# One recorded order for all engines up to the sixth MoE position

## The chip, the core and the metric

The kernel runs on one NeuronCore of a Trainium2 chip. The core has five engines that work side by side, each through its own list of instructions in order: TensorE (PE, matrix products and transposes; its weight loads are shown apart as PEld), VectorE (DVE), ScalarE (ACT), GpSimd (POOL) and SyncE (SP), which here issues all DMA transfers. The engines wait for each other through semaphores. The metric is the time of one execution on the device in microseconds; lower is better.

## What is computed

Banded attention over 2 batches, 8 heads, 768 positions of 64, and then two feed-forward layers over 1536 tokens. All of it is float32.

```python
k_sum = k.reshape(B, H, nb, 32, D).max(axis=3)     # 24 block maxima of K
v_sum = v.reshape(B, H, nb, 32, D).mean(axis=3)    # 24 block means of V
scores_l = scale * q @ k.T, kept where |i - j| < 16
scores_s = scale * q @ k_sum.T + log(32)
a = softmax(concat(scores_l, scores_s)) ; attn = a @ concat(v, v_sum)
x = attn as [1536, 512]
x = ((x @ w_a) * (x @ w_b)) @ w_out                # d_ff 1536, "moe"
h = x @ w_in ; out = (h - tanh(h)) @ w_out2        # d_ff 2048, "moe2"
```

The two weight sets arrive as 8-byte words per element (512 KB for a unit of 128 x 512 weights) and are turned into float32 on the chip.

## The kernel before

**Attention units.** The attention is cut into 24 units of 64 positions (all heads), 12 per batch. A unit's steps are T1 (transpose q, one T1 for two units), W (copy the band of 96 keys and the 24 block maxima into one tile), T2 (scores on TensorE, minimum and mask on VectorE, exponentials on ScalarE), T2b (divide by the sum), T3 (transpose the weights) and T4 (outputs on TensorE; ScalarE writes the high half into the x tile, VectorE subtracts for the low half). Eight units fill the x tile of one token block of 512.

**MoE positions.** The first feed-forward layer runs as a list of positions, `pos`, for three token blocks: for each of 12 groups f of 128 columns there is a product a (`pos_a`, 12 matmuls), a product b (`pos_b`, 12 matmuls, then VectorE multiplies a by b) and, one group later, an output product o (`pos_o`, 12 matmuls into four accumulators). The list begins a0 b0 a1 b1 o0 a2 b2 o1 a3. Each float32 operand is split in a high and a low half, and a product is made of three matmuls: gh and gl are the halves of a times b, and `wsp` holds those of a weight. Twelve matmuls of 128 x 512 belong to a position.

**Weights.** A position needs one weight unit. A unit is loaded into a buffer (three `stage` buffers, and x21a and x21b), decoded and split. The decode is two operations on ScalarE (`dec_a`: da and db), a clamp on GpSimd (dc), and a shift-and-mask (dd), a merge (de) and an add (df) on VectorE; the split is a copy on ScalarE (sh) and a subtraction (sl). When the add is done the buffer is free, and the next unit's load is issued on the SP queue.

**What sets the order.** The start is a recorded order: the string `SEQ` lists the steps of units 0 to 7 of the attention and the decodes and splits of the first three weights, and `op()` writes each step's instructions; `tc.manual_schedule` keeps them as they stand on each engine. A second recorded part follows for all engines but TensorE (loads for units 8 to 10 and `W(8)` to `W(11)`, two early key chunk loads). From position 0 on, `run_plan(j)` adds the planned steps of position j (decodes, attention of later units, key chunks of the second batch, V chunks), weights are split three positions ahead, and a scheduler orders the instructions of all engines but SP, whose order is kept as written up to position 72.

Names in the rows: XA and XB are the x tiles, kt the transposed keys, `w` and `vw` are pools of small tiles, ps, pt, pa, pb and acc are banks of the matmul memory. Lines of the page are those of the kernel before: L370 is in `proj` (products a and b), L398 in `pos_o`, L184 and L185 the split, L161, L164 and L165 dd, de and df, and L755, L757 and L759 the same steps in the recorded part; L601 is a copy on VectorE in the recorded part, L672 its masked minimum, L685 and L686 the sums, L720 and L722 the output halves; L386 multiplies a by b, L363 and L364 write gh and gl; L223, L269, L327 and L340 are the transposes of key chunks, T1, T3 and the outputs T4 of units from 8 on; L141 and L143 load weights, L258 loads V for a unit.

## Time and profile before

| what | before |
|---|---|
| median of three runs | 659.42 us (659.05 to 659.43) |
| the profiled execution | 659.97 us, span 658.2 us |
| TensorE busy | 637.4 us, 97% of the span |
| VectorE busy | 501.9 us, 76% |
| ScalarE busy | 475.1 us, 72% |
| GpSimd busy | 209.1 us, 32% |
| DMA traffic | 62.11 MB, 94 GB/s on average |

The profile is of one execution, by the hardware profiler, so it stands beside the median of the runs and not for it. Busy is the time that an engine's instructions took; matmuls overlap and their ends are modelled. A wait is put down to the engine whose result came last. The clock column of a stretch is the TensorE clock that was granted, as a share of full speed.

### The profile page before, as it was taken

How to read it: one execution, taken by the hardware profiler on the slowest of the kernel's cores; microseconds unless marked ns; L12 is line 12 of the kernel's file. 1: busy time of each engine (PE TensorE's matmuls, PEld its weight loads, DVE VectorE, ACT ScalarE, POOL GpSimd, SP SyncE). 2: the span in 40 equal slices, each digit the busy share in tenths (PEclk: the TensorE clock that was granted, in tenths of full speed). 3: DMA queues.
4: the chain of work that ended last, by engine and by line, in shares of the span. 5: the costliest groups of instructions: out<-in, count | busy, mean ns of one | idle time of the engine just before them, and what ended most of it. 6: DMA issues, size and time to landing. Idle time of an engine off the chain costs nothing.

```text
span 658.2 us, 9626 instructions
## 1 busy us (share of the span) xinstructions
PE 637.4 (97%) x3240; PEld 518.2 (79%) x3240; DVE 501.9 (76%) x999; ACT 475.1 (72%) x1000; POOL 209.1 (32%) x221
## 2 busy tenths in 40 slices
PE   7779999999799999999999999999999999999997
PEld 5567876888588888888888888888888888888885
DVE  5889999898675777747877749777777877777775
ACT  4899886897686787645655548777777777777774
POOL 6752231222000011100111134554444554444441
PEclk9979999999999999999999999999999999999999
DMA  9996984563324554513444200000010000010001
GB/s 203 242 240 185 249 224 127 176 214 116 81 89 124 164 161 141 154 54 113 143 145 145 80 1 0 1 0 1 1 64 1 0 1 0 26 40 1 1 0 64
DMA packets 84781, 62.11 MB, mean 94 GB/s; under 512 B 51892, under 2 KB 75444, under 8 KB 84732
## 3 DMA queue, kind: packets, MB, share of 16 engines
q1 hardware_dynamic: 84732, 61.50, 33.3%
q8 instruction: 25, 0.41, 0.3%
q14 instruction: 24, 0.20, 0.1%
HBM read 54.00 MB, written 7.34 MB: 93 GB/s over the span
## 4 chain that ended last, share of the span: by engine, by line
PE 83%; DVE 8%; ACT 4%; DMA 2%; issue 2%; SPq 1%; POOL 0%; DVEq 0%; ACTq 0%
PE acc L459 20%; PE pb L370 18%; PE pa L370 17%; PE acc L398 12%; PE pt L370 5%; PE ps L370 5%; PE ps L288 1%; DVE w L164 1%; PE ps L340 1%; DVE wsp L185 1%; DMA stage<-in_moe_w_in_dram 1%; DVE w L165 1%; PE pt L240 1%; PE pt L327 1%; SPq L610 1%
## 5 line engine op out<-in xcount | busy, mean ns | idle before, releaser
L185 POOL TENSOR_TENSOR wsp<-w,wsp 128x512 fp32r<-128x512 f32 x97 | 127.4, 1330 | 140.0 <-ACT wsp L184 140.0
L184 ACT ACTIVATE wsp<-w 128x512 fp32r<-128x512 f32 x201 | 121.3, 622 | 17.8 <-PE acc L398 8.0
L185 DVE TENSOR_TENSOR wsp<-w,wsp 128x512 fp32r<-128x512 f32 x104 | 73.9, 712 | 41.0 <-ACT wsp L184 40.8
L179 POOL TENSOR_SCALAR w<-w 128x512 f32<-128x512 f32 x52 | 41.8, 809 | 181.7 <-ACT w L154 168.9
L398 PE MATMUL acc<-gh,wsp 128*128 128x512 f32 x288 | 96.5, 394 | 1.2 <-ACT gh L363 1.2
L370 PE MATMUL pa<-XA,wsp 128*128 128x512 f32 x336 | 85.2, 402 | 2.1 <-ACT XA L720 2.1
L370 PE MATMUL pb<-XA,wsp 128*128 128x512 f32 x336 | 83.9, 393 | 1.4 <-DVE tg L386 1.4
L459 PE MATMUL acc<-wsp,gh 128*128 128x512 f32 x256 | 78.8, 389 | 0.0
L370 PEld LDWEIGHTS pa<-XA,wsp 128*128 128x128 f32 x336 | 64.1, 193 | 16.6 <-ACT XA L720 2.4
L370 PEld LDWEIGHTS pb<-XA,wsp 128*128 128x128 f32 x336 | 62.1, 188 | 14.9 <-ACT x21a L155 1.7
L363 ACT ACTIVATE gh<-tg 128x512 fp32r<-128x512 f32 x68 | 42.4, 624 | 33.9 <-DVE tg L386 33.6
L398 PEld LDWEIGHTS acc<-gh,wsp 128*128 128x128 f32 x288 | 53.7, 188 | 11.9 <-ACT gh L363 1.3
L370 PE MATMUL pb<-XB,wsp 128*128 128x512 f32 x240 | 60.8, 396 | 0.0
L370 PE MATMUL pa<-XB,wsp 128*128 128x512 f32 x240 | 60.0, 394 | 0.0
L398 PE MATMUL acc<-gl,wsp 128*128 128x512 f32 x144 | 56.8, 396 | 1.1 <-DVE gl L364 1.1
L459 PEld LDWEIGHTS acc<-wsp,gh 128*128 128x128 f32 x256 | 48.1, 188 | 9.9
L364 DVE TENSOR_TENSOR gl<-tg,gh 128x512 fp32r<-128x512 f32 x68 | 46.8, 688 | 9.1 <-ACT gh L363 8.9
L370 PEld LDWEIGHTS pa<-XB,wsp 128*128 128x128 f32 x240 | 44.5, 188 | 9.4 <-DVE XB L348 0.2
L370 PEld LDWEIGHTS pb<-XB,wsp 128*128 128x128 f32 x240 | 44.4, 188 | 9.2
L459 PE MATMUL acc<-wsp,gl 128*128 128x512 f32 x128 | 49.8, 389 | 0.0
L459 PE MATMUL acc<-wsp,vw 128*128 128x512 f32 x192 | 46.5, 391 | 0.0
L459 PEld LDWEIGHTS acc<-wsp,vw 128*128 128x128 f32 x192 | 35.9, 188 | 8.2 <-ACT vw L363 0.4
(304 smaller groups left out, 1175.5 us busy)
## 6 DMA issues: line engine op xcount, KB each, us to landing
stage<-in_moe_w_out_dram SPq DMA_DIRECT2D x19, 512.0 KB, 3.5
stage<-in_moe_w_in_dram SPq DMA_DIRECT2D x16, 512.0 KB, 5.6
stage<-in_moe_w_a_dram SPq DMA_DIRECT2D x8, 512.0 KB, 5.0
w<-wsc SPq DMA_DIRECT2D x16, 256.0 KB, 3.4
vw<-in_v_dram SPq DMA_DIRECT2D x19, 192.0 KB, 3.0
stage<-in_moe_w_b_dram SPq DMA_DIRECT2D x7, 512.0 KB, 5.6
wsc<-x21a SPq DMA_DIRECT2D x8, 256.0 KB, 5.1
wsc<-x21b SPq DMA_DIRECT2D x8, 256.0 KB, 4.9
```

The lines of the kernel that those rows point to most:

```text
L164: nc.vector.scalar_tensor_tensor(r, t[:, :, 1], -0x40000000, r, op0=ALU.bitwise_and, op1=ALU.bitwise_or)
L165: nc.vector.tensor_tensor(r, r, t[:, :, 0], op=ALU.add)
L179: nc.gpsimd.tensor_scalar(rf, rf, HI_HI, HI_LO, op0=ALU.min, op1=ALU.max)
L184: nc.scalar.activation(s[:, 0, :], r, AF.Copy)
L185: eng.tensor_tensor(s[:, 1, :], r, s[:, 0, :].bitcast(F32), op=ALU.subtract)
L240: mm(pp, mavg[:, NB - 4 - 4 * c : 2 * NB - 4 - 4 * c], vch.pop(c).rearrange("p h d -> p (h d)"), start=(c == 0), stop=(c == NC - 1),)
L288: mm(pp[:, p, 0:NK], qt[:, p, :], kw[:, p, :], start=True, stop=True)
L363: nc.scalar.activation(dst[0], src, AF.Copy)
L364: eng.tensor_tensor(dst[1], src, dst[0].bitcast(F32), op=ALU.subtract)
L370: mm(dst, w, xx, start=(kk == 0 and n == 0), stop=(kk == KC - 1 and n == 2))
L398: mm(acc[blk][d][:, c0:c1], w, t, start=(f == 0 and c0 == 0 and n == 0), stop=(f == F1 - 1 and n == 2))
L459: mm(a[c], g[:, cs], s[:, i, :], start=(f == 0 and n == 0), stop=(f == F2 - 1 and n == 2))
```

## The change

The recorded part becomes longer and holds all engines, TensorE too. `HEAD_P = 6` positions (a0 b0 a1 b1 o0 a2) are written out as steps M0 to M5 with their evictions (Ma copies a product a, Mt multiplies a by b, Mh and Ml write gh and gl). `HEAD_W = 10` weights are decoded there instead of three, and splits are recorded for the first nine instead of three. Units 8 and 9 of the attention are in the recorded order (unit 9 up to its division), and so are the first three key chunks of the second batch (KP transposes, KE copies, KR takes maxima) and the loads Lk, Lc (V chunks) and LV8 to LV11. The scheduler takes over at position 6.

Besides the order, some steps go to another engine. The copies of the block means of V for units 0 to 7 (`VCE`) were two on ScalarE, two on VectorE and four on GpSimd, and are five on VectorE and three on GpSimd. The add of the decode (`ADD`) was on GpSimd for the first weight, and now is for the second and third; the split's subtraction (`SPL`) was on GpSimd for two weights, and now is for three. W(8) to W(11) stood together on ScalarE ahead of the first product; W(8) and W(9) now stand near the start and W(10) and W(11) among the products.

On the SP queue the first q tile is issued ahead of the last K tile, the first weight (Lw0) right behind the second q tile, and the second weight behind the three V tiles. A buffer that a decode frees is no longer reloaded at once: its name goes into `freed`, and the step Lw with the next number issues the load where it stands in the order.

```diff
     HALF, WARM, VM, PK, KS = 0, 3, 3, -3, 2
+    HEAD_W, HEAD_P = 10, 6
...
-    REG = {0:{ET.SP},72:None}
+    REG = {6:{ET.SP},72:None}
...
     for i, u in enumerate(dseq):
-        if i < LOOK:
+        if i < HEAD_W:
             continue
...
-        plan(ja, dec_a, u)
-        plan(ja + 1, dec_b_next, i)
+        plan(max(ja, HEAD_P), dec_a, u)
+        plan(max(ja + 1, HEAD_P), dec_b_next, i)
...
     for c in range(NC):
-        plan(PK + KS * c, lambda c=c: load_k(1, c, st([128, H, D], "w", 3 * F1)))
-        plan(PK + KS * c + 4, prep_k, 1, c, "ps" if c % 2 else "pt")
+        if c == 5:
+            plan(PK + KS * c, lambda c=c: load_k(1, c, st([128, H, D], "w", 3 * F1)))
+        if c >= 3:
+            plan(PK + KS * c + 4, prep_k, 1, c, "ps" if c % 2 else "pt")
...
-    T3E, WE, ADD, SPL, VCE = 'DDDDADDD', 'PPDPPDPP', 'PDD', 'PPD', 'APPPAPDD'
+    T3E, WE, ADD, SPL, VCE = 'DDDDDDAD', 'DPDPPPPP', 'DPPDDDDDDD', 'PPPDDDDDD', 'DDDDDPPP'
...
+        elif k == "M":
+            fn, g, u = pos[i]
+            x, sp = X[0], wsp.pop(u)
+            if fn is pos_o:
+                fn(g, sp)
+            else:
+                P_["M", i] = pt("pa" if fn is pos_a else "pb")
+                proj(P_["M", i], sp, x)
+        elif k == "Ma":
+            j = (0, 2, 5)[i]
+            ab[pos[j][1]] = st([128, TB], "ta", 2)
+            nc.scalar.activation(ab[pos[j][1]], P_["M", j], AF.Copy)
+        elif k == "Mt":
+            j = (1, 3)[i]
+            vp["t", i] = st([128, TB], "tg", 2)
+            nc.vector.tensor_tensor(vp["t", i], P_["M", j], ab.pop(pos[j][1]), op=ALU.mult)
...
         elif k == "Lw":
-            load_next(("stage", "stage", "stage", "x21a", "x21b")[i])
+            load_next(("stage", "stage", "stage", "x21a", "x21b")[i] if i < 5 else freed[i - 5])
...
                 EN[ADD[i]].tensor_tensor(r, r, t[:, :, 0], op=ALU.add)
-                load_next(staged.pop(u)[1])
+                freed[i] = staged.pop(u)[1]
...
-    with tc.manual_schedule(engines=set(ET_HEAD)):
-        load_q(4)
-        load_v(8)
-        for u in range(8, 12):
-            W(u)
-        load_v(9)
-        load_v(10)
-        for j in range(-12, 0):
-            run_plan(j)
     reg = ExitStack()
     for j, (fn, i, u) in enumerate(pos):
+        if j < HEAD_P:
+            assert j not in at
+            continue
```

The string `SEQ` itself is replaced; what that does to the engines is seen in their lists. Line numbers differ between the two programs: L601 of before is L609 of the change, L672 is L731, L685 and L686 are L744 and L745, L755 and L757 are L820 and L822.

VectorE in the middle of the softmax, between the minima of units 0 to 7 and the first outputs (sm is a unit's sum, the COPY rows bring transposed weights and block means of V out, `w<-w 128x512` is a decode's shift-and-mask and `w<-stage,w` its merge). Before:

```order
L685 TENSOR_SCALAR sm<-sm 128x4
L686 RECIPROCAL sm<-sm 128x4
L601 COPY gh<-acc_427 120x512
L601 COPY gh<-acc_436 120x512
L685 TENSOR_SCALAR sm<-sm 128x4
L686 RECIPROCAL sm<-sm 128x4
L601 COPY w<-acc_446 120x512
L601 COPY vw<-w 24x512
L601 COPY gl<-ps 120x512
```

And with the change, in the same part:

```order
L820 TENSOR_SCALAR w<-w 128x512
L609 COPY gh<-pb 120x512
L822 SCALAR_TENSOR_TENSOR w<-stage,w 128x512
L744 TENSOR_SCALAR sm<-sm 128x4
L745 RECIPROCAL sm<-sm 128x4
L609 COPY at<-acc_457 120x512
L609 COPY w<-w 24x512 x5
L609 COPY gh<-ps 120x512
```

The second weight's decode now stands between these rows (the first one's stands further ahead, between the minima), and five copies of the block means stand in one place.

TensorE at the first MoE products (L370 are products a into pa and b into pb, L398 an output product; the rest are steps of units 8 and 9 and of the key chunks). Before:

```order
L269 MATMUL pt<-ident,w 128x128 x4
L370 MATMUL pa<-XA,wsp 128x512 x12
L288 MATMUL ps<-w,qbd 128x120 x4
L223 MATMUL pt<-ident,w 128x128 x4
L370 MATMUL pb<-XA,wsp 128x512 x2
L370 MATMUL pa<-XA,wsp 128x512 x12
L370 MATMUL pb<-XA,wsp 128x512 x10
L223 MATMUL ps<-ident,w 128x128 x4
L370 MATMUL pb<-XA,wsp 128x512 x12
L327 MATMUL pt<-ident,e 120x128 x4
L370 MATMUL pa<-XA,wsp 128x512 x12
```

With the change (L774 are outputs of units up to 8, L761 transposed weights of units up to 8):

```order
L774 MATMUL pb<-w,vw 64x64 x8
L288 MATMUL ps<-w,qbd 128x120 x4
L370 MATMUL pa<-XA,wsp 128x512 x12
L370 MATMUL pb<-XA,wsp 128x512 x12
L370 MATMUL pa<-XA,wsp 128x512 x12
L370 MATMUL pb<-XA,wsp 128x512 x12
L761 MATMUL pt<-ident,e 120x128 x4
L398 MATMUL acc_817<-gh,wsp 128x512
L398 MATMUL acc_817<-gl,wsp 128x512
```

The scores of units 8 and 9 have moved ahead of the first product, the key chunks behind the fifth position, and four positions stand without a step between. Further on, the outputs of unit 10 stand behind 215 MoE matmuls where they stood behind 202.

VectorE up to the low half gl of the second group (`tg<-pb,ta` is a times b). Before:

```order
L386 TENSOR_TENSOR tg<-pb,ta 128x512
L226 TENSOR_REDUCE kt<-ps 128x4x4
L364 TENSOR_TENSOR gl<-tg,gh 128x512
L161 TENSOR_SCALAR w<-w 128x512
L185 TENSOR_TENSOR wsp<-w,wsp 128x512
L164 SCALAR_TENSOR_TENSOR w<-stage,w 128x512
L161 TENSOR_SCALAR w<-w 128x512
L364 TENSOR_TENSOR gl<-tg,gh 128x512
```

With the change, the rows from the second product (L659) to the second gl (L666):

```order
L659 TENSOR_TENSOR tg<-pb,ta 128x512
L787 TENSOR_TENSOR XB<-ps,XB 128x4x64
L161 TENSOR_SCALAR w<-w 128x512
L744 TENSOR_SCALAR sm<-sm 128x4
L164 SCALAR_TENSOR_TENSOR w<-stage,w 128x512
L745 RECIPROCAL sm<-sm 128x4
L640 TENSOR_REDUCE kt<-pt 128x4x4
L165 ISA w<-stage,w 128x1024
L752 TENSOR_TENSOR e<-e,sm 128x480
L185 TENSOR_TENSOR wsp<-w,wsp 128x512
```

Behind these stand one more shift-and-mask and one reduction of a key chunk, and then the gl. Steps of unit 8 and 9 and of the eleventh weight now stand between the second product and its gl, where before one split, two decode steps and the first group's gl stood.

## Rows read from the trace of the kernel before

**Rows 1.** The page: span and TensorE's line.

```profile
span 658.2 us, 9626 instructions
PE 637.4 (97%) x3240; PEld 518.2 (79%) x3240; DVE 501.9 (76%) x999; ACT 475.1 (72%) x1000; POOL 209.1 (32%) x221
```

**Rows 2.** Stretches: length, busy us of PE, PEld, DVE, ACT, POOL; granted clock; DMA.

```profile
7.35:17.00 9.65, 7.10 (x53) 5.70 (x52) 8.07 (x30) 5.58 (x15) 4.22 (x14) 1.00 1.31 237
7.35:42.48 35.13, 25.26 (x267) 19.58 (x265) 29.63 (x117) 27.75 (x99) 22.25 (x34) 0.99 1.08 232
42.48:57.37 14.89, 13.43 (x53) 10.32 (x53) 14.40 (x30) 13.83 (x32) 5.30 (x6) 0.80 0.98 241
57.37:74.18 16.81, 16.81 (x96) 13.88 (x97) 15.96 (x37) 14.64 (x35) 3.37 (x4) 1.00 0.75 198
74.18:168.00 93.82, 93.82 (x509) 73.62 (x507) 83.58 (x191) 78.04 (x180) 23.59 (x27) 1.00 0.61 173
168.00:177.00 9.00, 5.56 (x52) 3.89 (x52) 8.20 (x17) 5.59 (x15) 0.00 (x0) 1.00 0.31 83
177.00:650.00 473.00, 473.00 (x2241) 390.85 (x2240) 345.86 (x605) 331.52 (x641) 148.64 (x127) 1.00 0.18 59
```

**Rows 3.** TensorE's waits, whole run: total, times, longest, in us.

```profile
PE pa L370 <- ACT XA L720: 2.1, 1, 2.1
...
PE acc L398 <- ACT gh L363: 1.2, 1, 1.2
...
PE acc L398 <- DVE gl L364: 1.1, 1, 1.1
PE ps L340 <- ACT at L330: 1.0, 1, 1.0
PE pt L269 <- DVE XA L722: 0.9, 1, 0.9
```

**Rows 4.** Timeline of TensorE: the first product and the ninth position.

```profile
42.48 5.74 PE L370 MATMUL pa<-XA,wsp 128*128 128x512 f32 x12 [2.11 <-ACT XA L720]
...
74.18 2.88 PE L370 MATMUL pa<-XA,wsp 128*128 128x512 f32 x12
```

**Rows 5.** VectorE's waits from 7 to 75 us: total, times, longest.

```profile
DVE sm L685 <- ACT tg L680: 2.4, 1, 2.4
DVE XA L722 <- ACT XA L720: 1.0, 1, 1.0
```

**Rows 6.** The chain that ended last, 70 to 90 us: start, length.

```profile
74.34 2.72 PE pa L370 x12
77.07 0.44 PE pt L327 x4
```

**Rows 7.** Timeline of VectorE, the third gl.

```profile
73.19 0.68 DVE L364 TENSOR_TENSOR gl<-tg,gh 128x512 fp32r<-128x512 f32 x1
```

**Rows 8.** VectorE's groups by form, 0 to 75 us: busy, mean ns.

```profile
L161 DVE TENSOR_SCALAR w<-w 128x512 int32<-128x512 int32 x8 | 4.4, 553 | 0.0
L757 DVE SCALAR_TENSOR_TENSOR w<-stage,w 128x512 int32<-128x512 int32 x3 | 2.8, 934 | 0.1
L164 DVE SCALAR_TENSOR_TENSOR w<-stage,w 128x512 int32<-128x512 int32 x4 | 2.8, 689 | 0.0
...
L165 DVE CUSTOM_DVE_ANT_0 w<-stage,w 128x1024 uint16<-128x1024 uint16 x3 | 2.1, 688 | 0.0
L386 DVE TENSOR_TENSOR tg<-pb,ta 128x512 f32<-128x512 f32 x3 | 2.1, 686 | 0.3 <-PE pb L370 0.3
...
L299 DVE CUSTOM_DVE_ANT_0 e<-ps,mask 128x120 f32<-128x120 f32 x8 | 1.8, 276 | 0.0
...
L601 DVE COPY vw<-w 24x512 f32<-24x512 f32 x2 | 1.2, 616 | 0.1
```

**Rows 9.** Timelines of SP and ScalarE: the weight behind unit 10's V load.

```profile
110.46 0.42 SPq L141 DMA_DIRECT2D x21a<-in_moe_w_a_dram  x1
...
115.88 0.67 ACT L154 ACTIVATE w<-x21a 128x512 f32<-128x512 f32 x1 [1.92 <-DMA x21a<-in_moe_w_a_dram]
```

More of the change, by code (lines that the diff above doesn't have):

```diff
@@ L517, in band_attention_moe_kernel @@
     dseq = order[:nw1] + early + order[nw1 + 1 :: 2]
-    at = {}
+    at, vt2 = {}, {}
     def plan(j, fn, *args):
@@ L647, in op @@
         elif n.startswith("T1e"):
-            i, o = int(n[3]), "ab".index(n[4])
-            qt = qbs[i]
-            x = slice(o * 64, o * 64 + 64)
-            cp("AD"[o], qt[x, :, :, x], P_["T1", i][x].rearrange("x p (u c) -> x u p c", u=2))
+            i = int(n[-1])
+            qt = qbd if i == 4 else qbs[i]
+            for o in range(2) if i == 4 else ("ab".index(n[3]),):
+                x = slice(o * 64, o * 64 + 64)
+                cp("A" if i == 4 else "AD"[o], qt[x, :, :, x], P_["T1", i][x].rearrange("x p (u c) -> x u p c", u=2))
             for r in range(2):
@@ L688, in op @@
             e, nm, sm = at_x[i]
-            nc.gpsimd.tensor_tensor(e, e, sm.unsqueeze(2).to_broadcast([128, NP, NK]), op=ALU.mult)
+            if i == 8:
+                for p in range(NP):
+                    nc.scalar.activation(e[:, p, :], e[:, p, :], AF.Copy, scale=sm[:, p : p + 1])
+            else:
+                (nc.vector if i == 9 else nc.gpsimd).tensor_tensor(
+                    e, e, sm.unsqueeze(2).to_broadcast([128, NP, NK]), op=ALU.mult
+                )
             at_x[i] = e
```

76 lines of the change are left out of this document (57 added, 19 removed).

## The prediction, made before the changed kernel was run

> **What bounds the kernel now.** I read the page first. TensorE is busy for 97% of the span [rows 1], so the question is where it stands still. A table of stretches answers that. Before the first MoE product, from 7.35 to 42.48 us, TensorE is busy for 25.3 of 35.1 us. From 42.48 to 57.37 it is busy for 13.4 of 14.9 us at a mean granted clock of 0.80. From 57.37 to 168 us it has no hole at all, between 168 and 177 us it has one (5.56 busy of 9.00, so 3.4 us lost), and from 177 to 650 us it is full again [rows 2]. So every microsecond by which the full stretch starts earlier comes off the end, as long as nothing later makes TensorE wait. The waits by engine name what ends at the hole at 168 us: the halves gh and gl and the tile at, products of ScalarE and VectorE [rows 3].
>
> Which engine sets the start of the full stretch? VectorE. Over 7.35 to 74.18 us its busy time is 29.63 + 14.40 + 15.96 = 59.99 us of 66.83 [rows 2], so it stood still for only 6.84 us. ScalarE, by the same rows, is busy for 27.75 + 13.83 + 14.64 = 56.2 and has 10.6 us of slack. The waits of VectorE show where its larger idle pieces lie: 2.4 us for exponentials and 1.0 us for the last attention output [rows 5]. The opening up to 17 us holds 9.65 - 8.07 = 1.58 us of idle time [rows 2].
>
> I take the start of the ninth position (the product a of the fourth f group) as the finish line, since before and after have nearly the same set of work behind them there. Before, it starts at 74.18 us [rows 4]. In the new order TensorE has also done two groups of four transposes by then (unit 9's T3 and the fourth key chunk), 0.44 us each [rows 6]. The mark to beat is therefore 74.18 + 0.88 = 75.06 us.
>
> **The change part by part.** *The decode and split work* of the first ten weights does not shrink. It moves ahead, into gaps of the softmax stretch. What VectorE has to finish before TensorE can leave the second o position is the low half gl of the second group. In the new list the rows up to that gl hold, against the rows of before up to its third gl at 73.19 us [rows 7], one more shift-and-mask (0.55 us), one more merge (0.69), three more copies of the mean of V, which leave ScalarE and GpSimd (3 x 0.62), and one product and one gl less (2 x 0.69) [rows 8]. Adds and split subtractions on VectorE come out even (nine and seven in both). Sum: 0.55 + 0.69 + 1.86 - 1.38 = +1.7 us. So VectorE needs 59.99 + 1.7 = 61.7 us of work, and that gl cannot end before 7.35 + 61.7 = 69.05 us.
>
> Behind that gl, TensorE has eight products of 0.227 us (2.72 us for twelve) and the two groups of transposes, together 1.8 + 0.9 = 2.7 us [rows 6]. With no idle moment of VectorE the finish line would be at 69.05 + 2.7 = 71.75 us, 3.3 us ahead of the mark. With all the idle time of before, 6.84 us, it would be at 78.6, 3.5 us behind. These are the two bounds of the idle term.
>
> I choose 1.58 us, the idle time of the opening, because the K and q loads that cause it keep their place at the head of the queue, and it is the piece that no new filling touches. The 2.4 us wait goes: decode steps now stand in that stretch of VectorE's list. The 1.0 us wait goes for the larger part: the eight copies for units 8 to 11 that stood on ScalarE ahead of the last output pair now stand partly at the start and partly far behind it. Result: 71.75 + 1.58 = 73.3 us, 1.73 us ahead of 75.06.
>
> *TensorE itself* is not the limit of the head. The first product needs all eight output pairs. VectorE's list up to them is longer than before by three copies (1.86 us), the scores of unit 8 (four operations of the form that takes 0.28 us, some 0.9 us together) and one more decode (0.55 + 0.69 + 0.69) [rows 8], 4.7 us in all. The idle time saved is 5.3 us in total, most of it ahead of this place, so the first product starts at about 43 us against 42.48 [rows 4]. From there TensorE has 96 products (21.8 us) and eight small groups (3.5 us) up to the finish line: 68.3 us at the earliest. VectorE's 73.3 leaves it 5.0 us of slack.
>
> [...]
>
> *The two early weight loads* (one behind the second q tile, one behind V's first three) put twice 512 KB ahead of other loads. ScalarE's first decode stands in its list ahead of the first exponential and waits for the first of these. I cost it at nothing, because the first exponential waits for scores anyway; if the load lands late, each microsecond goes straight into the idle term, whose upper bound holds it. The key chunks and loads of units 8 to 10 move behind weight loads on the SP queue; in the head only the chunks' own transposes and unit 8's outputs wait for them.
>
> *After the head* both programs have the same rows per position. In the stretch from 74.18 to 168 us VectorE is busy for 83.58 us of 93.82 [rows 2], so it can hold a lead. The hole of 3.4 us at 168 us stays as it is, since the order of loads there is unchanged; its bounds are nothing and twice its size.
>
> The sum is made on the profiled execution, 659.97 us for a span of 658.2 [rows 1]: 659.97 - 1.73 = 658.24. That execution lies 0.55 us above the median of 659.42, so against the median I forecast 657.7 us.
>
> [...] GpSimd works for 22.25 + 5.30 + 3.37 us of the head [rows 2], and the merge on VectorE takes 0.93 us on average in the first three decodes, beside GpSimd's work, against 0.69 for four others [rows 8]: 0.24 us lost in each. [...] The sum goes by the rows' busy times, in which such losses are already contained at the rate of before.
>
> **The rivals.**
> *Slower: collisions in the denser head.* Decode steps now lie beside GpSimd's normalisations, adds and splits, from 16 to 50 us. For it: 0.93 against 0.69. Against it: GpSimd's own list is only some 2 us longer. If each of 25 such steps loses another 0.24 us, VectorE ends 6.0 us later, and the finish line is at 79.3, 4.2 us behind the mark: 663.6 us. It decides from 1.7 + 1.3 = 3.0 us on, thirteen such losses more than before. Chance 0.20. [...]
>
> *The gain is given back at the loads of V.* On the SP queue a load of V for unit u+3 waits for unit u's output products, and weight loads stand behind it. Unit 10's products come after 202 MoE products before and after 215 in the new order, 13 x 0.227 = 3.0 us later within the work. Before, the weight behind that load was issued at 110.46 us and ScalarE waited 1.92 us for it at 115.88 [rows 9], and TensorE did not wait. If 1 to 2 of the 3.0 us reach TensorE, the gain is gone: 659.4 us. For it: ScalarE works in order, and a gh stands behind the wait. Against it: that gh is wanted two positions (5 us) later. Chance 0.20.
>
> *Better: VectorE without idle time, or a hole at 168 us that closes in part.* 3.3 us and up to 3.4 more: 656.1 down to 652.7 us. Chance 0.15.
>
> **How the numbers follow.** The forecast, a finish line between 71.8 and 74.6 us and nothing lost later, has 0.45 and reaches from 656.1 to 659.0 us. A measurement of this kernel tells about 0.2%, 1.3 us, from no change, so faster ends at 658.1 and slower begins at 660.7. Faster: 0.15 for the better case and 0.35 of the forecast's 0.45, together 0.50. Same: the 0.10 left of the forecast and 0.20 for the gain given back, 0.30. Slower: 0.20. For 8 in 10 the range takes in most of the better case and half of the slower one: 654.0 to 662.0 us.
>
> **What would show it.** In the new profile, VectorE's idle time from its first K reduction to the second gl should be 1 to 3 us, its busy time about 62 us, and the 2.4 us wait gone. The fourth product a should start at about 73 us, and TensorE should wait in the head for the second group's gl. [...] From the finish line to 168 us TensorE should be full. I am wrong if VectorE's busy time up to that gl is above 64 us (collisions), if TensorE has holes between 100 and 150 us behind late weights, or if the hole at the block's end has another size than 3.4 us.

## The result and the profile after

| | before, same job | changed kernel |
|---|---|---|
| first job | 659.42 us (659.05 to 659.44) | 669.09 us (666.27 to 671.35), ratio 1.0145 [1.0097, 1.0193] |
| second job, same kernel again | 659.58 us | 665.94 us (665.36 to 670.58), ratio 1.0089 [1.0073, 1.0106] |

The change makes the kernel slower, by about 0.9 to 1.5%, where the prediction had 657.7 us. The first job's profiled execution took 1067.16 us, at a mean granted clock of 0.558 (see the last section), and one execution of the kernel before took 1295.36 us, at 1.000; both are left out of the medians and ratios here. The rows are of the second job's profile: 670.58 us, 4.6 above that job's median. Its mean granted clock is 0.982, that of the four unprofiled executions 0.991 to 0.992, so the sizes of half-clock stretches in it are at the upper end, and the median execution must lose less than it somewhere.

The page, lines that answer to [rows 1]:

```profile
span 668.9 us, 9613 instructions
PE 644.2 (96%) x3240; PEld 523.8 (78%) x3240; DVE 501.6 (75%) x1000; ACT 473.1 (71%) x998; POOL 211.4 (32%) x222
```

Stretches, with the columns of [rows 2]: the opening; up to the first product; up to the second gl, the place to which the prediction summed VectorE's work; two short stretches; from the fourth product a to 178 us; and the hole:

```profile
7.35:17.00 9.65, 7.26 (x55) 6.13 (x54) 8.52 (x33) 6.39 (x14) 3.86 (x13) 1.00 1.30 246
7.35:47.40 40.05, 29.86 (x284) 25.27 (x283) 35.22 (x131) 28.99 (x99) 25.84 (x35) 0.87 1.01 206
7.35:81.82 74.47, 58.67 (x407) 46.97 (x406) 62.66 (x185) 54.04 (x159) 35.99 (x46) 0.86 0.97 213
59.19:62.60 3.41, 3.41 (x10) 2.48 (x9) 3.01 (x6) 2.74 (x6) 1.13 (x1) 0.50 1.29 203
72.85:79.67 6.82, 5.65 (x16) 4.59 (x17) 5.45 (x12) 5.58 (x16) 0.67 (x2) 0.50 1.05 263
84.61:178.00 93.39, 93.39 (x517) 73.16 (x516) 78.20 (x187) 75.68 (x180) 19.61 (x25) 1.00 0.53 156
178.00:187.00 9.00, 6.22 (x27) 4.13 (x27) 7.90 (x15) 5.27 (x10) 0.00 (x0) 0.81 0.30 83
```

The two other falls of the clock in the head, and the stretch from the first output to the first product:

```profile
21.40:25.00 3.60, 3.54 (x18) 3.29 (x17) 2.56 (x13) 3.28 (x17) 1.07 (x2) 0.53 1.16 303
35.30:42.10 6.80, 4.90 (x48) 4.61 (x50) 6.66 (x15) 3.92 (x12) 3.67 (x5) 0.50 0.73 180
37.20:47.40 10.20, 10.20 (x157) 9.31 (x157) 9.66 (x29) 6.20 (x15) 6.54 (x7) 0.76 0.34 100
```

TensorE's timeline, with the rows that answer to [rows 4]: outputs of the units, the first product, the second b, the third a, a group of transposes of a key chunk, the third b, and the fourth a:

```profile
37.20 1.12 PE L774 MATMUL pt<-at,w 120*64 120x64 f32 x16 [3.85 <-DMA vw<-in_v_dram]
47.40 3.02 PE L370 MATMUL pa<-XA,wsp 128*128 128x512 f32 x12
58.26 4.60 PE L370 MATMUL pb<-XA,wsp 128*128 128x512 f32 x12 [1.93 <-DVE tg L659]
67.42 2.98 PE L370 MATMUL pa<-XA,wsp 128*128 128x512 f32 x12
74.02 1.12 PE L635 MATMUL pt<-ident,w 128*128 128x128 f32 x4 [3.61 <-DVE kt L640]
74.79 5.26 PE L370 MATMUL pb<-XA,wsp 128*128 128x512 f32 x12
84.61 3.00 PE L370 MATMUL pa<-XA,wsp 128*128 128x512 f32 x12
```

The fourth product a starts at 84.61 us against the mark of 75.06: 9.55 us late. Behind it lie 668.9 - 84.61 = 584.3 us, before 658.2 - 75.06 = 583.1. So 9.55 of the 10.7 us between the two spans arise in the head. VectorE's work up to the second gl is 62.66 us (predicted 61.7); its idle time is 74.47 - 62.66 = 11.81 us (predicted 1.58). Against the predicted 73.3 us the fourth product a is 11.3 us late: 10.2 us of that are idle time and 1.0 us is work. The loss is waiting, and the place where most of it ends last is the third b, where TensorE stands for 3.61 us and then runs at the lower clock level (granted 0.50) from 72.85 to 79.67 us.

Following that wait back takes three engines. VectorE's timeline (in brackets, the idle time ahead of a row and its releaser): the copy of the fourth transposed q tile (for units 6 and 7), and the maxima (L640) of the first and of the third key chunk:

```profile
22.34 0.69 DVE L609 COPY wsp<-acc 64x512 f32<-64x512 f32 x1 [2.71 <-ACT wsp L607]
...
73.27 0.69 DVE L640 TENSOR_REDUCE kt<-pt 128x16 f32<-128x512 f32 x1 [4.20 <-ACT kt L638]
...
80.52 0.69 DVE L640 TENSOR_REDUCE kt<-ps 128x16 f32<-128x512 f32 x1 [1.79 <-PE ps L635]
```

ScalarE, with the two steps of the eleventh weight's decode (L154, L155) and the copy of the first key chunk (L638):

```profile
68.03 0.36 ACT L785 ACTIVATE XB<-ps 128x256 fp32r<-128x256 f32 x1
71.55 0.66 ACT L154 ACTIVATE w<-stage 128x512 f32<-128x512 f32 x1 [3.15 <-DMA stage<-in_moe_w_out_dram]
72.11 0.66 ACT L155 ACTIVATE stage<-stage 128x512 int32<-128x512 uint32 x1
72.66 0.58 ACT L638 ACTIVATE kt<-pt 128x512 f32<-128x512 f32 x1
```

The SP queue, where that weight's load is the last row:

```profile
54.91 0.37 SPq L141 DMA_DIRECT2D x21b<-in_moe_w_b_dram  x1
55.37 3.08 SPq L258 DMA_DIRECT2D vw<-in_v_dram  x3
58.51 2.73 SPq L214 DMA_DIRECT2D w<-in_k_dram  x2
61.28 2.53 SPq L252 DMA_DIRECT2D w<-in_q_dram  x2
63.85 1.13 SPq L214 DMA_DIRECT2D w<-in_k_dram  x1
65.08 0.97 SPq L143 DMA_DIRECT2D stage<-in_moe_w_out_dram  x1
```

Read from the queue back up: eight loads of V, K and q stand between the tenth weight's load and the eleventh's. The eleventh is issued at 65.08 us, and ScalarE stands 3.15 us for it, until 71.55. The first key chunk had been transposed on TensorE from 67.01 us on, but its copy stands behind that decode in ScalarE's list. VectorE's maxima wait 4.20 us for the copy, TensorE's next transposes 3.61 us for the maxima (they reuse the bank pt), and the third b stands behind these transposes. ScalarE kept to the order of its list here: the copy, whose input was there, began at 72.66 us, behind a decode that had waited 3.15 us for an input that was not.

### The profile page after: what moved, and what is told of

It reads as the page before. It is cut to its first block, busy times and chain, and to the rows that moved or that the text cites. A ratio compares the mean times of both kernels' runs of the same rounds, so it can differ in the third digit from the quotient of the medians.

```text
span 1065.4 us, 9613 instructions
## 1 busy us (share of the span) xinstructions
PE 1055.1 (99%) x3240; PEld 623.7 (59%) x3240; DVE 501.9 (47%) x1000; ACT 484.4 (45%) x998; POOL 203.5 (19%) x222
## 2 busy tenths in 40 slices
DMA packets 84781, 62.11 MB, mean 58 GB/s; under 512 B 51892, under 2 KB 75444, under 8 KB 84732
## 3 DMA queue, kind: packets, MB, share of 16 engines
HBM read 54.00 MB, written 7.34 MB: 58 GB/s over the span
## 4 chain that ended last, share of the span: by engine, by line
PE 96%; DVE 2%; ACT 1%; DMA 0%; issue 0%; SPq 0%; ACTq 0%
PE pb L370 21%; PE pa L370 21%; PE acc L459 21%; PE acc L398 15%; PE ps L370 5%; PE pt L370 5%; PE ps L288 2%; PE ps L340 1%; PE pt L327 1%; PE pt L240 1%; PE pt L269 1%; DMA stage<-in_moe_w_in_dram 0%; PE ps L840 0%; DVE kt L690 0%; PE acc L774 0%; DVE sm L744 0%
## 5 line engine op out<-in xcount | busy, mean ns | idle before, releaser
L398 PE MATMUL acc<-gh,wsp 128*128 128x512 f32 x288 | 147.2, 583 | 0.0
L370 PE MATMUL pa<-XA,wsp 128*128 128x512 f32 x336 | 136.9, 578 | 0.0
L370 PE MATMUL pb<-XA,wsp 128*128 128x512 f32 x336 | 136.4, 577 | 0.0
L459 PE MATMUL acc<-wsp,gh 128*128 128x512 f32 x256 | 123.2, 577 | 0.0
L370 PEld LDWEIGHTS pb<-XA,wsp 128*128 128x128 f32 x336 | 72.7, 218 | 54.3 <-issue 32.6
L370 PEld LDWEIGHTS pa<-XA,wsp 128*128 128x128 f32 x336 | 73.7, 221 | 52.6 <-issue 29.7
L370 PE MATMUL pb<-XB,wsp 128*128 128x512 f32 x240 | 99.5, 582 | 0.0
L370 PE MATMUL pa<-XB,wsp 128*128 128x512 f32 x240 | 98.2, 577 | 0.0
L398 PEld LDWEIGHTS acc<-gh,wsp 128*128 128x128 f32 x288 | 63.6, 222 | 42.6 <-issue 24.0
L398 PE MATMUL acc<-gl,wsp 128*128 128x512 f32 x144 | 83.9, 582 | 0.0
L459 PE MATMUL acc<-wsp,vw 128*128 128x512 f32 x192 | 76.8, 574 | 0.0
L370 PEld LDWEIGHTS pa<-XB,wsp 128*128 128x128 f32 x240 | 52.3, 221 | 36.7 <-issue 21.5
L459 PE MATMUL acc<-wsp,gl 128*128 128x512 f32 x128 | 73.7, 576 | 0.0
L370 PEld LDWEIGHTS pb<-XB,wsp 128*128 128x128 f32 x240 | 52.2, 219 | 36.1 <-issue 21.1
L386 DVE TENSOR_TENSOR tg<-pb,ta 128x512 f32<-128x512 f32 x34 | 23.5, 691 | 93.5 <-PE pb L370 92.4
```

What stands on the lines that cost most here:

```text
L370: mm(dst, w, xx, start=(kk == 0 and n == 0), stop=(kk == KC - 1 and n == 2))
L386: nc.vector.tensor_tensor(t, p, ab.pop(g), op=ALU.mult)
L398: mm(acc[blk][d][:, c0:c1], w, t, start=(f == 0 and c0 == 0 and n == 0), stop=(f == F1 - 1 and n == 2))
L459: mm(a[c], g[:, cs], s[:, i, :], start=(f == 0 and n == 0), stop=(f == F2 - 1 and n == 2))
```

## The experiments

In the table, "first" is the start of the first product and "fourth a" that of the fourth product a in the profiled execution; VectorE's busy and idle time run from its first maximum of K (6.97 to 7.36 us) to the second gl. Ratios are to runs of the kernel before on the same chip. The change's own ratio was 1.0145 [1.0097, 1.0193] in the first job; the runs are set against the second job's, whose interval is the narrower. A profile is one execution, so places in it that differ by 1 us or less are not told apart.

| run | median us | ratio, 95% | first | fourth a | VectorE busy / idle |
|---|---|---|---|---|---|
| change (after_again) | 665.94 | 1.0089 [1.0073, 1.0106] | 47.40 | 84.61 | 62.66 / 11.81 |
| e1_t1_first | 665.44 | 1.0082 [1.0066, 1.0099] | 45.82 | 81.40 | 63.33 / 7.91 |
| e2_loads_early | 670.30 | 1.0156 [1.0141, 1.0171] | 48.38 | 82.32 | 64.52 / 8.47 |
| e3_both | 667.83 | 1.0106 [1.0086, 1.0125] | 45.88 | 80.99 | 64.97 / 6.30 |
| e4_no_clamp | 662.74 | 1.0052 [1.003, 1.0074] | 47.58 | 78.11 | 59.48 / 8.93 |
| e5_decode_behind | 671.45 | 1.0159 [1.012, 1.0197] | 48.60 | 85.16 | 63.39 / 9.73 |
| e6_decode_behind_t1 | 668.67 | 1.0119 [1.0084, 1.0154] | 45.27 | 83.70 | 64.09 / 6.28 |
| e7_behind_no_clamp | 664.17 | 1.0051 [1.0028, 1.0075] | 48.10 | 78.10 | 61.13 / 6.82 |
| e8_behind_t1b | 668.04 | 1.0098 [1.0066, 1.0131] | 46.84 | 83.73 | 64.17 / 7.26 |
| e9_both_chunks_ahead | 666.22 | 1.0081 [1.0059, 1.0104] | 48.77 | 81.96 | 61.24 / 9.08 |
| e10_ahead_t1_loads | 663.25 | 1.0049 [1.0032, 1.0067] | 45.86 | 78.20 | 62.11 / 5.12 |
| e11_no_clamp_same_list | 666.95 | 1.0111 [1.0079, 1.0144] | 47.25 | 78.67 | 60.93 / 8.03 |
| e12_fill_the_gap | 664.53 | 1.0063 [1.0045, 1.0081] | 46.22 | 78.14 | 62.23 / 5.74 |
| e13_product_early | 665.14 | 1.0074 [1.0062, 1.0087] | 47.01 | 80.19 | 62.28 / 6.83 |
| e14_product_and_gh_early | 664.75 | 1.0071 [1.0051, 1.009] | 45.60 | 78.68 | 61.63 / 6.06 |
| e15_copies_on_act | 662.46 | 1.0039 [1.0025, 1.0054] | 45.81 | 77.90 | 60.35 / 7.75 |
| e16_all_lists | 663.66 | 1.0065 [1.0042, 1.0088] | 44.95 | 76.76 | 59.51 / 6.63 |
| e17_loads_and_ahead | 665.12 | 1.0073 [1.0052, 1.0093] | 46.61 | 78.97 | 60.94 / 7.34 |

**after_again**, the change once more.

> The changed kernel, unchanged, for a second trace and a second set of times. Theory 1 (the clock): TensorE's granted clock falls to its lower level for longer in the head than before (before: one fall of 6.8 us), and the extra time at the lower level, halved, is the 7 to 12 us that the kernel loses; the time is 666 to 671 us. Rival (VectorE): the clock shows the same single fall of about 7 us, and the fourth product a starts 4 us or more later than 75 us, with VectorE busy for more than 64 us up to the second gl. A third way (one bad measurement): the time is 656 to 660 us.

It is slower again, and its profile is the one read above. None of the three ways holds as written. VectorE is busy for 62.66 us, below 64, and the fourth a is late all the same. The clock does not fall once, for about 7 us as before, but four times in the head and once at the hole. How long an execution stood at the lower level can be estimated from its mean clock, with 1.00 and 0.50 for the two levels as in the stretches above: (1 - 0.982) x 2 x 668.9 = 24 us in this profile, 11 to 12 us in the four other executions of the job (0.991 to 0.992), about 6.6 us at the median clock of the kernel before in that job (0.995). Halved, since products of 128 x 512 started 0.43 us apart at 0.50 and 0.23 at 1.00 (kernel before: 45.46 to 46.74 us, and the twelve of [rows 6]), the difference between the typical executions is 2 to 3 us of the 6.4 between the medians, so the clock alone does not make the loss. In the profile, 1.8 of VectorE's 11.81 us of idle time end at TensorE in one piece (the row at 80.52).

### The waits one at a time

**e1_t1_first** moves both halves of the copy of the fourth q tile (T1ea3 on ScalarE, T1eb3 on VectorE) ahead of the exponentials of unit 2; VectorE's half had waited 2.71 us for ScalarE's. The rest of the first weight's decode moves up behind them.

```diff
-T1t3 dc0 ex2 T1ea3 T2m5 ex1 T1eb3 dd0 rb2 T2m4 tt5 de0 df0 Lv2
+T1t3 T1eb3 T1ea3 dc0 ex2 T2m5 ex1 dd0 de0 df0 tt5 rb2 T2m4 Lv2
```

> The changed kernel with ScalarE's and VectorE's halves of the fourth q eviction ahead of the exponentials of unit 2, and a decode between them and that unit's reciprocals. Theory A (the idle term: VectorE bounds the first product, and the 2.71 us wait for this eviction took the place of the 2.4 us wait that the change removed): the 2.7 us wait is gone, the first product starts 1.0 to 2.7 us ahead of 47.4 us. The time falls by that only if the late weight at 71.5 us is not what decides afterwards: 664 to 666 us if it counts, 666 to 669 us if it does not. Rival B (the loads of V set the first output product, as the wait at 37.2 us is labelled): the outputs start at 37.2 us as before, the first product stays at 47 us.

The 2.71 us wait went, and VectorE's idle time fell by 3.9 us. The outputs started at 35.24 us instead of 37.20 with the same loads; their wait (3.27 us) is now put down to VectorE's copy. None of the three loads into `vw`, issued from 29.29 us on and landing 6.0 us later or more, had landed by then. So the load of V that the row at 37.20 names was not its releaser, and does not hold the first outputs up. No gain is seen at the end: 1.0082 against 1.0089. By the two profiles the fourth a came 3.2 us earlier, but the change's profile lies 4.6 us above its job's median and e1's 0.5.

**e2_loads_early** moves four of the eight loads ahead of the sixth weight, where the SP queue stood still; **e3_both** is e1 and e2 together.

```diff
-... df1 Lw5 dc3 ... LV9 LV10 Lk0 dc5 ... sl4 Lk1 sl6 ... db8 Lq5 Lq6 T3t8 ...
+... df1 Lw5 Lk0 Lk1 Lq5 Lq6 dc3 ... LV9 LV10 dc5 ... sl4 sl6 ... db8 T3t8 ...
```

> The changed kernel with two key chunks and two q tiles issued on the SP queue behind the sixth weight, into the stretch from 36 to 45 us where the queue stood still, and not behind the tenth weight at 58 to 65 us. Theory A (the burst of loads between the tenth and the eleventh weight delays the eleventh; ScalarE waits 3.15 us for it with the first key chunk's eviction behind it, VectorE waits 4.2 us for that, TensorE 3.6 us, and TensorE's clock then falls): the eleventh weight lands before 68.5 us, these waits are gone, the second product b of a group follows its product a without a gap, no half clock at 73 to 80 us, and the time is 659 to 663 us. Rival B (the eleventh weight is late because its buffer comes free late, with the sixth decode at 64 us): the waits shrink by 1 us at most, 665 to 670 us.

> Both edits together. Theory A: the first product starts 1.0 to 2.7 us ahead of 47.4 us, and the wait for the eleventh weight is gone: 656 to 661 us, so the head is no worse than before. Rival B: nothing adds up, because GpSimd's collisions with VectorE or TensorE's clock set the head; 664 us or more.

In e2 the eleventh weight was issued at 60.15 us instead of 65.08, right behind an add of a decode that ended at 60.12; in the change the same add ended at 59.14, so there it was the burst of loads that held the issue back, and not a buffer (rival B). The wait for the weight was cut; the fourth a came 2.3 us earlier in e2 and 3.6 in e3. Yet neither run is faster than the change. That they are slower is not shown: e3's interval overlaps that of the change, and e2's 1.0156 lies above the second job's interval but inside the first job's. TensorE then waited elsewhere: 0.9 us ahead of the third a in both, and 1.4 us ahead of the third b in e2. The scheduler, which takes over at the sixth position, ordered the rest differently, and behind the fourth a both take 586 us, against 584.3 in the change and 583.1 before. The early loads alone do not mend it.

### The places of the decodes

**e5_decode_behind** records the eleventh weight's decode behind the first key chunk's copy (HEAD_W = 11); **e6_decode_behind_t1** adds e1's edit, **e8_behind_t1b** another order of the same copies, and **e7_behind_no_clamp** is e5 without the clamps of the recorded decodes.

```diff
-    HEAD_W, HEAD_P = 10, 6
+    HEAD_W, HEAD_P = 11, 6
...
-... KE0 KR0 ex9 Mt1 T4l8 rb9 Lw13 Lc2 M5 Mh1 KP2 KR2 nm9 KE2 ... Lw14 Ml1
+... KE0 KR0 ex9 Mt1 T4l8 rb9 Lw13 Lc2 M5 Mh1 da10 db10 dc10 dd10 KP2 KR2 de10 df10 nm9 KE2 ... Lw14 Lw15 Lc3 Ml1
```

> The changed kernel with the eleventh weight's decode inside the fixed list, behind the first key chunk's eviction and the tenth unit's exponentials on ScalarE; the loads stand as they were. Theory A2 (in-order ScalarE: the first key chunk's eviction stood behind a decode whose weight had not landed): VectorE's 4.2 us wait and TensorE's 3.6 us wait at 70 to 74 us are gone although the weight lands as late as before, the clock does not fall there, and the time is 661 to 663.5 us against 665.9. Rival C (GpSimd's clamps slow VectorE, and leaving them out was what gave the run without clamps its 662.7): 665 us or more here. Rival D (another late weight takes the place at the second key chunk): the wait comes back at 76 to 80 us, 664 to 667 us.

> As the one with the decode behind, and the fourth q eviction ahead of the exponentials of unit 2. Theory A: the first product starts at 45.8 us and not at 47.4 us, and, with the wait behind it gone, the 1.0 to 1.6 us reach the end: 660 to 662.5 us. Rival: a later wait takes them up again, no difference to the one without it.

> As the one with the decode behind, without the clamps of the first ten weights (left out of the decode). If GpSimd's collisions with VectorE cost time on the path: 2 to 3 us less than with the clamps. If they lie beside other waits: within 1 us of it.

> As the one with the decode behind and the fourth q eviction early, and the third q tile's eviction starts with ScalarE's half, ahead of the reciprocal. ScalarE stood idle there for 1.2 us and TensorE for 2.1 us: the scores of unit 5 start 0.4 us earlier, the first product at 45.4 us, and the time is that of the one before less 0 to 0.4 us.

In e5 the third b came at 71.69 us, right behind its a at 68.51, so the wait of the change was gone. The next copy of a key chunk then stood behind the next weights. ScalarE's timeline in e5:

```profile
76.74 0.68 ACT L154 ACTIVATE w<-stage 128x512 f32<-128x512 f32 x1 [0.93 <-DMA stage<-in_moe_w_b_dram]
...
77.89 0.57 ACT L638 ACTIVATE kt<-pt 128x512 f32<-128x512 f32 x1
```

and TensorE's, the transposes of a unit's q:

```profile
78.51 0.65 PE L269 MATMUL pt<-ident,w 128*128 128x128 f32 x4 [2.43 <-ACT kt L638]
```

TensorE's 2.43 us here took the place of the 3.61: moving one decode only hands the wait to the next copy, and the fourth a came no earlier (85.16). Against e5, e6 and e8 moved the first product ahead by 3.3 and 1.8 us and the fourth a by 1.5 and 1.4, without a difference in the ratio that can be told from the change. e7 is faster than e5 (1.0051 against 1.0159, intervals apart), but in it the scheduler also put the later chunk's copy ahead of the next decodes, so clamps and places changed together there.

**e9_both_chunks_ahead** records twelve decodes, the eleventh and twelfth behind the copies of both chunks.

```diff
-    HEAD_W, HEAD_P = 10, 6
+    HEAD_W, HEAD_P = 12, 6
...
-... M5 Mh1 KP2 KR2 nm9 KE2 KP1 KR1 KE1 LV11 Ma2 Lw14 Ml1
+... M5 Mh1 KP2 KR2 KE2 da10 db10 dc10 dd10 nm9 KP1 KR1 KE1 LV11 Ma2 Lw14 Ml1 da11 db11 dc11 de10 dd11 df10 Lw15 Lc3 de11 df11 Lw16
```

> The changed kernel with the decodes of the eleventh and twelfth weight in the fixed list behind the evictions of the first two key chunks on ScalarE; loads as they were. Theory A3 (the weights behind the burst of loads land at 71.5, 74 and 76 us, and whatever stands behind their decodes on ScalarE waits, which one only depends on the list): TensorE has no wait over 1 us between the products a and b of the third group nor in the second o position, the fourth product a starts before 80 us (84.6 before, 85.2 with one chunk ahead), and the time is 661 to 664 us. Rival: the weights themselves are wanted by then, the wait moves to the splits and the fourth product, 665 to 670 us.

The third waiter: now the thirteenth weight's decode stands ahead of a copy of q for units 10 and 11. ScalarE's timeline in e9:

```profile
77.44 0.68 ACT L155 ACTIVATE stage<-stage 128x512 int32<-128x512 uint32 x1 [2.25 <-DMA stage<-in_moe_w_b_dram]
```

and TensorE's, behind it:

```profile
79.25 0.65 PE L327 MATMUL pt<-ident,e 128*120 128x128 f32 x4 [2.11 <-ACT qbd L273]
```

**e10_ahead_t1_loads** is e9 with the edits of e1 and e2; **e17_loads_and_ahead** is e9 with e2's alone.

> All three edits: chunk evictions ahead of late decodes, the fourth q eviction early, key chunks and q tiles loaded in the stretch where the queue stood still. Theory A3: first product at 45.5 to 46 us, no waits of over 1 us from there to the fourth product a, which starts at 77 to 78.5 us (75.1 is the level of the kernel before): 660 to 662 us. Rival: the loads' move costs 2 us behind the head, as it did alone: 662 to 665 us.

> As the run with all three edits (e10), with the q eviction of unit 1 left where the change has it, behind the exps. Theory (the loads and the places of the decodes are what counts at the fourth product, and the 2.71 us wait at 22 us is made up behind it): fourth product a at 79.5 to 80.5 us, ratio 1.005 to 1.006. Rival (the 2.7 us wait is passed on to the end of the head in full): fourth product a at 80.9 us or later, ratio 1.008 to 1.010.

e10 is 1.0049, and its interval [1.0032, 1.0067] lies apart from the change's [1.0073, 1.0106]. Windows of e10, up to the first product and up to the second gl:

```profile
7.35:45.86 38.51, 30.12 (x282) 25.27 (x281) 35.89 (x131) 28.78 (x99) 24.80 (x35) 0.87 1.20 243
...
7.35:74.58 67.23, 56.06 (x406) 44.86 (x404) 62.11 (x182) 52.93 (x158) 34.24 (x44) 0.90 1.10 236
```

VectorE's idle time is down from 11.81 to 5.12 us with the same work, and the third b stands at 68.97 us right behind its a at 65.79. The fourth a starts at 78.20, 3.14 us behind the mark, and the median is 3.02 us above its 660.23 of before: place and time agree. From its first product to its fourth a e10 takes 32.34 us; before, 74.18 - 42.48 + 0.88 = 32.58. By TensorE's rows, what is left of the loss therefore lies ahead of the first product, at 45.86 against 42.48. In e17 the 2.71 us wait is back and the fourth a comes 0.8 us later than in e10, so by the profiles most of it is made up behind; its ratio of 1.0073 can be told neither from e10's nor from the change's.

### Collisions: the clamps left out

**e4_no_clamp** leaves out the clamp of the recorded decodes, GpSimd's part of them (ten operations). **e11_no_clamp_same_list** leaves them out too, but records the eleventh decode ahead of the first chunk's copy, as the change has it on ScalarE.

```diff
             if k == "dc":
-                clamp(u)
+                clamped.add(u)
```

> The changed kernel without the clamps of the first ten weights on GpSimd (it leaves out that part of the decode). Collision theory (GpSimd's work beside VectorE's costs it 9.0 us in 20 to 60 us against 5.4 us in the kernel before): VectorE's operations in that stretch lose 3 us less, the first product is 2 to 3 us earlier. Theory of the late load: the eleventh weight still comes at 70 to 71.5 us and the time gains less than 2 us, 665 to 668 us. If collisions decide, 660 to 663 us.

> Without the clamps of the first ten weights (left out of the decode), but with the eleventh weight's decode ahead of the first key chunk's eviction, as in the changed kernel. If the place of that decode made the run without clamps faster: the wait is back in part (the weight is issued 1.5 us earlier without clamps), 664 to 667 us. If GpSimd's clamps were the cost: 662 to 663.5 us as before.

e4, at 1.0052 [1.003, 1.0074], lies below the change, the two intervals just touching, and taken alone it speaks for the collisions. But without clamps the scheduler had put the first chunk's copy at 68.30 us, ahead of the decode. With the place held, in e11, the ratio is 1.0111 [1.0079, 1.0144], no better than the change's. TensorE's timeline in e11, where the wait ahead of the third b is still there (the profile names no releaser, which it calls issue):

```profile
70.97 0.63 PE L635 MATMUL pt<-ident,w 128*128 128x128 f32 x4 [3.08 <-issue]
```

VectorE's work fell by 1.7 us (60.93 against 62.66) without the clamps, and the time did not follow. In the head it did: the second b waited 0.55 us instead of 1.93, and the fourth a came at 78.67, 5.9 us ahead of the change's and within 0.6 us of e4's 78.11. e11 gives it back behind the head (664.3 - 78.67 = 585.6 us). So e4 and e11 differ in time without differing at the fourth a, and which part of e4's gain is the place and which the clamps is not shown.

### What bounds the rest

**e12_fill_the_gap** is e10 with 16 transposes of the identity that nothing reads, ahead of the second b, so that TensorE does not stand still there.

```diff
-... df6 dc7 M3 dd7 ...
+... df6 dc7 dx4 M3 dd7 ...
```

> The version with all three edits, with 16 transposes of the identity matrix into a free bank between the second product a and the second product b (1.75 us at the higher level, in the 1.93 us that TensorE waits there for tg). If the fall of TensorE's clock at 58 to 61 us follows from that wait: no half clock there, the product b takes 2.8 us and not 4.5 us, the time falls by 1 to 1.7 us to 661.5 to 662.3 us. If the fall comes from something else: it stays, and the time is the same or up to 0.5 us longer, 663.2 to 663.8 us.

A window of e10 around 60 us:

```profile
58.13:61.55 3.42, 3.42 (x12) 2.35 (x11) 3.38 (x6) 3.42 (x9) 1.48 (x1) 0.50 1.31 231
```

TensorE's timeline of e10, the second b:

```profile
56.72 4.32 PE L370 MATMUL pb<-XA,wsp 128*128 128x512 f32 x12 [1.93 <-DVE tg L659]
```

The same window of e12:

```profile
58.00:62.00 4.00, 3.56 (x15) 2.06 (x13) 4.00 (x7) 3.66 (x10) 1.12 (x1) 1.00 1.26 251
```

TensorE's timeline of e12, the second b and the first product with gl:

```profile
57.11 3.03 PE L370 MATMUL pb<-XA,wsp 128*128 128x512 f32 x12 [0.21 <-DVE tg L659]
...
62.41 0.50 PE L398 MATMUL acc<-gl,wsp 128*128 128x512 f32 x1 [0.84 <-DVE gl L666]
```

With the gap filled the clock stayed at 1.00 and the b took 3.03 us instead of 4.32. TensorE then waited 0.84 us for gl, and the fourth a came at 78.14 against 78.20. So in these two runs the fall went with the wait: with 1.93 us of it the clock stood at 0.50 for 3.42 us, with 0.21 us of it the clock did not fall. In this place no cost of the fall is seen at the fourth a, and e12's ratio (1.0063) is no lower than e10's; VectorE and ScalarE are all but full over the fall in e10 (3.38 and 3.42 of 3.42 us).

**e13_product_early** is e10 with the first a times b ahead of tt9, a division by GpSimd; **e14_product_and_gh_early** also writes gh and gl earlier.

```diff
-... db6 da7 tt9 ... LV8 sl3 de6 sl2 Mt0 M2 ...
+... db6 da7 Mt0 sl3 tt9 ... LV8 de6 sl2 M2 ...
```

> The version with all three edits, with the first product of the halves (tg) and the fourth weight's low half ahead of unit 9's scores and a decode in VectorE's list. Theory (what is left of the loss lies in waits of TensorE for rows that stand too far back in in-order lists): the 1.93 us wait is gone, with it the half clock at 58 to 61 us; but the first o position still waits for gh and gl behind the tenth weight's decode on ScalarE, so part of it comes back there: 660.5 to 663 us. Rival (VectorE's total work bounds the head): no change, 663 to 664 us.

> As the one before, and gh and the normalisation of unit 8 stand ahead of the tenth weight's decode on ScalarE (which waited 2.7 us for its load there), gl behind the fifth weight's low half on VectorE. Theory: the first o position starts 2 to 3 us earlier, the fourth product a at 75 to 77 us (75.1 is the level of the kernel before), 658.5 to 661 us. Rival (VectorE's total work bounds the head): the wait moves to the third product a for its weight's low half, the fourth product a stays at 78 us, 663 us.

The 1.93 us wait of the second b went in both, and came back elsewhere: in e13 as 2.6 us for weights of the attention (L761), in e14 as 1.6 and 0.9 us for unit 8's outputs and a copied product. Neither is faster than e10.

**e15_copies_on_act** is e10 with three of the five VectorE copies of the block means on ScalarE; **e16_all_lists** is e15 with e14's edits and one more copy, of transposed weights, on ScalarE.

```diff
-    ... VCE = ... 'DDDDDPPP'
+    ... VCE = ... 'DAADAPPP'
```

> The version with all three edits, with three of the five copies of the mean of V moved from VectorE to ScalarE (ScalarE waits 2.95 us there). If VectorE's amount of work bounds the head: its work up to the second gl falls from 62.1 to 60.3 us, the first product starts 1 to 1.8 us ahead of 45.9 us, the fourth product a at 76.5 to 77.5 us, and the time is 661 to 662.5 us. If not (ScalarE bounds as well, or another wait takes its place): the fourth product a stays at 78 us, 663 us.

> All edits together: loads, chunk evictions ahead of late decodes, the early q eviction, product and gh early, three copies and one more eviction of the transposed attention on ScalarE. If VectorE bounds: work of 59.7 us up to the second gl, as much as before, and the fourth product a at 76 to 77 us, within 2 us of the level of the kernel before: 660.5 to 662 us. If the rows behind the head that the scheduler places differently cost 1 to 2 us, as they did with the product early: 662 to 664 us.

Window of e15 up to the first product:

```profile
7.36:45.81 38.45, 29.22 (x283) 24.54 (x282) 34.31 (x128) 30.67 (x102) 24.52 (x35) 0.91 1.20 243
```

VectorE has 1.58 us less work there than in e10 (34.31 against 35.89), and the first product did not move (45.81 against 45.86): its idle time took the whole of it. e15's 1.0039 is the lowest ratio of all, and cannot be told from e10's. The traces show what stands there in VectorE's place. Window of e15 from the first output to the first product:

```profile
35.56:45.81 10.25, 10.25 (x156) 9.36 (x157) 7.86 (x26) 7.04 (x17) 6.27 (x7) 0.75 1.11 241
```

The same of e16:

```profile
35.51:44.95 9.44, 9.44 (x156) 8.65 (x157) 7.34 (x25) 7.55 (x18) 6.43 (x7) 0.83 1.10 244
```

TensorE does not stand still in either, with the same 156 matmuls. Behind its wait of 3.3 to 3.4 us for the first output the clock is at its lower level, by an estimate from the mean clock for (1 - 0.75) x 2 x 10.25 = 5.1 us of this stretch in e15 and for 3.2 us in e16; less half of that the two take about the same, 7.7 and 7.8 us. So by these rows it is TensorE at the lower clock that ends last ahead of the first product in e15, and not VectorE's 7.86 us of work. In the change the mean clock of that stretch is as low, 0.76, and VectorE, busy for 9.66 of 10.20 us there, stands close behind; up to the first product the mean clock is 0.87 in e10 as in the change. e16 brings the fourth a to 76.76, within 1.7 us of the mark, and gives it back behind the head, with a larger hole at 173 to 182 us. No order that was tried beats the kernel before.

## Why the prediction was wrong, step by step

- **The finish line** held. In the profile 9.55 of 10.7 us lie ahead of the fourth a, and from there to 178 us TensorE is full (93.39 of 93.39 us).
- **VectorE's work** held: 61.7 us predicted, 62.66 measured, below the 64 named as the sign of collisions. The collision rival had the direction right (slower, 663.6 us) but not the size, and its sign is not there. That the clamps cost nothing is not shown: e11 took 1.7 us off VectorE's work with the place held, its fourth a came earlier, and its time did not.
- **The idle term failed**: "I choose 1.58 us", measured 11.81, beyond even the upper bound of 6.84. The bound was the idle time of the old order, and nothing keeps a new order below it. Two waits named above make up 6.9 us, the 4.20 and the 2.71; the 1.79 behind TensorE's slow third b is the next. The first comes from the step "in the head only the chunks' own transposes and unit 8's outputs wait for them". The moved loads were checked for who waits for them, not for what they stand ahead of: the eleventh weight's load, and through ScalarE's list a key chunk, and through the bank pt the third b. The second wait stands against "The 2.4 us wait goes": a copy of q, in place of a sum, now stood behind exponentials. That they count when taken away together is shown by e10, whose idle time is 5.12 us; e1, e2, e5 and e9, one edit each, show no gain. In the medians, e10's three edits are worth about 0.4% (1.0089 to 1.0049).
- **The first product** was set at about 43 us and came at 47.40. VectorE's work ahead of it is 35.22 us against 29.63 [rows 2], 5.6 more, where the sum had 4.7. The idle time there is 40.05 - 35.22 = 4.83 us against 5.50, where the sum had taken some 4.2 us of it away. In e10 2.62 us of it are left, and work of 6.3 us more. "*TensorE itself* is not the limit of the head" also failed here: from the first output at 37.20 us to the first product TensorE shows no idle time, at a mean clock of 0.76.
- **Behind the second gl** 2.7 us were predicted, 84.61 - 81.82 = 2.79 measured.
- **The clock** fell more often than before. Instead of one fall of 6.8 us (before, 0.50 from 41.6 to 48.4 us) there were four in the head, at 21, 35, 59 and 73 us, of 3.4 to 6.8 us, each at a wait of TensorE of 1.9 to 3.9 us. That TensorE has slack in the head (5.0 us in the prediction) is right in kind for the one at 59 us, the only one that was tried (e12: the fourth a at 78.14 us without the fall, at 78.20 with it). The one at 35 us lies on the outputs, where TensorE has no slack. Behind the wait at 74.02 VectorE waited 1.79 us for TensorE's transposes, so there the slower third b (5.26 us) was probably on the path; no run separates this.
- **The two early weight loads** show no wait of their own. **Rival "given back at the loads of V"**: no sign of it, TensorE is full where it would lie. The wait at 37.20 us that names a load of V is VectorE's (e1).
- **The hole**: 3.4 us predicted as unchanged. In the change it stands at 178 us with 2.78 us idle, and a mean clock of 0.81: products behind it start 0.43 us apart (182.34 to 184.90 us), ahead of it 0.23 (174.93 to 176.52 us); together with what else differs behind the head it is 584.3 - 583.1 = +1.2 us.

Two things stay open. First, why e10 and e15 still lose 0.4 to 0.5%: the loss is the 3.4 us by which the first product is late, but e15 shows that VectorE's amount of work alone does not set that. In e15 TensorE waits 3.4 us there for a copy on VectorE, and then runs the outputs in part at the lower clock; half of that low time is 2.6 us. That is a candidate for most of the 3.4; it is not shown, since no run took this fall out by itself. Second, how much is lost behind the head in e2, e3, e4, e11 and e16 (585 to 588 us behind the fourth a, before 583.1): their recorded parts end differently, the scheduler orders what follows differently, and that part was never held fixed.

## What to carry to other kernels

When a load is moved later in a queue, list what now stands behind it as well as who waits for it, and follow each of these through the in-order lists of the engines to the one that bounds. The idle time of an old order is no upper bound for that of a new one: bound it by the waits that the new lists make possible, a late input at each decode ahead of a copy that TensorE needs. Taking away one wait in such a chain showed nothing here until its neighbours were moved too, so a single undo that changes nothing does not clear its suspect. And a wait of TensorE ahead of small products should be priced with the half clock that came behind it here (about 0.50 for 3.4 to 6.8 us, at waits of 1.9 to 3.9 us).

## What the runs showed of the hardware that was not expected

In the execution of 1067.16 us the granted clock of TensorE stood between the two levels of the other profiles, 0.50 and 1.00, from 8.9 us to the end. Its span and mean granted clock:

```profile
core 0: 1065.4 us, clock 0.558
```

A window of its middle, with the columns of [rows 2]:

```profile
100.00:1000.00 900.00, 899.29 (x2635) 523.51 (x2634) 404.49 (x762) 396.07 (x782) 148.74 (x141) 0.56 0.14 46
```

TensorE is shown busy for all but 0.7 of these 900 us, so this is no wait: matmuls of 128 x 512 started 400 ns apart instead of 227, and the granted share was 0.55 to 0.56 in every stretch that was read, down to stretches of 0.2 us. What sets it off is not known from these runs.

One and the same program does not stand at the lower level for the same time in each execution: by the estimate from the mean clock (0.982, and 0.991 to 0.992) the changed kernel did so for 24 us in its profile and for 11 to 12 us in the four other executions of that job.
